# Turning both heads of 72 attention units on VectorE, and reordering the halves' difference, the sums and the statistics, in a fused top-k attention and feed-forward kernel

## The chip, the cores and the metric

The kernel runs on one core of one Trainium2 chip. The metric is the device time of one execution in microseconds, the median of three runs. Names of engines: TensorE (PE in the profile, PEld for its weight loads), VectorE (DVE), ScalarE (ACT), GpSimd (POOL), SyncE (SP, which here issues nearly all transfers).

## What is computed

Top-k attention over 8 batches x 8 heads, 576 positions, 64 columns a head, and on its output a normalised two-layer network without further weights on the residual:

```python
scores = (1/sqrt(64)) * q @ k.T
kth = the 32nd largest score of each row
attn = softmax(where(scores >= kth, scores, -1e9))
x = attn @ v                      # (8, 8, 576, 64) -> (8, 576, 512)
xn = (x - mean(x)) / sqrt(var(x) + 1e-6) * g_ln
out = x + relu(xn @ w_ch1) @ w_ch2   # 512 -> 2048 -> 512
```

All of it is float32.

## The kernel before

**Units and steps.** Work is cut into 160 *units*: 128 queries (or the last 64, a "rest" unit that carries both heads in its 128 partitions) of one pair of heads of one batch. A batch has 20 units. From batch 2 on they come in groups of a pair of heads: units 0, 1 and the rest unit, for each of the four pairs; then units 2 and 3 for each pair. The program is a hand-written order: a loop over steps n, and in each step every engine gets its part of several units at once. In step n TensorE makes the scores of unit n+1, VectorE selects the top 32 of unit n, ScalarE masks unit n-1, and unit n-2 (`ex`) is exponentiated (`weigh`, line 452), turned and put into the group's buffer `pt`. One step after a group's last unit was turned, `values` (lines 563 and 570) multiplies `pt` with V; `place` scales and stores the result as rows of x (line 579), `stats` (lines 629 to 638) centres the rows, and the second network starts on them. Each engine takes its instructions in this written order.

**Selection.** From unit 8 on a unit is *halved*: `halve` (lines 375 to 377) compares the two halves of 288 scores of each row. VectorE writes the larger of each pair to `hi`, GpSimd the smaller to `lo`, by integer arithmetic on the bit patterns: a + b first, then minus `hi`. `lo` has one buffer, `hi` two. `select_halved` then takes the top 8 of `lo` twice (line 390, in part 0), appends them to `hi`, and takes the top 8 of `hi` four times (line 398, `match_replace` in line 385): once in part 1, once in part 2, twice in part 3. In a step the order on VectorE is: part 0 for unit n, part 1, `halve` of unit n+1, part 2, part 3. So part 0 of the next step is what reads `lo`. `sc`, the scores, has four buffers: the buffer that unit n-2 used is filled again with the scores of unit n+2, in step n+1 (line 335).

**Turning.** The product with V needs the weights transposed: keys in the partitions. TensorE does this by `transpose` of four 128 x 128 pieces of a head into PSUM (line 505), and ScalarE copies them to `pt` (line 517 for head 0, line 521 for head 1). The last 64 columns of both heads go the same way (lines 538 and 539). In 72 units (from batch 2 on, every unit that is neither a rest unit nor the last of its group; `moved`) head 1 takes another way: `move` (lines 482 to 489) lets VectorE turn 32 x 32 blocks of `e` into the old score buffer, stores that to HBM with one transfer and loads it back in four, rearranged, so that whole columns lie in the right partitions. The half of `pt` for head 1 is laid out in blocks of 32 queries for this (`ptB`). `move` stands after part 0 of the selection, and so ScalarE exponentiates head 1 first in these steps.

**The second network.** Its matmuls (`hidden`, line 680, and `project`, line 697) are items of a queue `todo`. At fixed places of a step `fill` takes so many from it as the step's `share` allows. Up to step 17 (`CONVERTING`), while the weights are still being converted from 64-bit numbers, the share is worked out from estimated costs (`dve_cost` less `pe_cost`); after that it is what is left to do, spread evenly over the steps up to the next block of rows.

**Small parts.** `prepare` (lines 436 and 437) makes the exponential's bias from the largest and the 32nd score: on VectorE up to unit 16, on GpSimd afterwards. Line 932 turns a group's sums into reciprocals. Line 188 shifts bits of the weights. Line 304 turns q and k. Line 710 on GpSimd adds the residual.

Of the kernel before, what the change touches and what calls it, by code (L numbers as in the profile page):

```python
# [10 lines left out]
ALU = mybir.AluOpType  # L11
FP32 = mybir.dt.float32
U32 = mybir.dt.uint32
I32 = mybir.dt.int32
# [7 lines left out]
J = 4  # L22
# [7 lines left out]
def kernel(  # L30
# [41 lines left out]
    nc = tc.nc  # L72
    P = nc.NUM_PARTITIONS
    B, H, S, D = q.shape
# [3 lines left out]
    JP = J * P  # L78
    R = S - JP
    NHP = H // 2  # L80
    scale = 1.0 / float(D) ** 0.5
# [281 lines left out]
    def halve(u):  # L363

        nt = len(u.tiles)  # L370
        u.lo = lopool.tile([P, 2, HALF], FP32, tag="lo", name="lo")
        u.hi = hipool.tile([P, 2, HALF + TOP_K // 2], FP32, tag="hi", name="hi")
        a, b = u.sc[:, 0:nt, 0:HALF], u.sc[:, 0:nt, HALF:S]
        lo, hi = u.lo[:, 0:nt], u.hi[:, 0:nt, 0:HALF]
        nc.gpsimd.tensor_tensor(lo.bitcast(I32), a.bitcast(I32), b.bitcast(I32), ALU.add)  # L375
        nc.vector.tensor_tensor(hi, a, b, ALU.max)  # L376
        nc.gpsimd.tensor_tensor(  # L377
            lo.bitcast(I32), lo.bitcast(I32), hi.bitcast(I32), ALU.subtract
        )

    def select_halved(u, i):
        nt = range(len(u.tiles))
# [46 lines left out]
    def prepare(u):  # L429

        nt = len(u.tiles)
        u.bias = small.tile([P, 2], FP32, tag="bias", name="bias")
        b = u.bias[:, 0:nt]

        engine = nc.vector if u.i < CONVERTING else nc.gpsimd
        engine.tensor_tensor(b, u.thr[:, 0:nt, 7], u.top[:, 0:nt, 0], ALU.subtract)  # L436
        engine.tensor_scalar(b, b, scale, 0.0, ALU.mult, ALU.add)  # L437

    def mask(u, t):
        if u.e is None:  # L440
# [5 lines left out]
    def weigh(u, t):  # L446
        g = u.group
        if g.den is None:
            g.den = denpool.tile([P, 2 * J + 1], FP32, tag="den", name="den")
        col = 2 * u.qt + t  # L450
        u.weighed += 1
        nc.scalar.activation(  # L452
            u.e[:, t], u.e[:, t], AF.Exp, bias=u.bias[:, t : t + 1], scale=-scale / SLOPE,
            accum_out=g.den[:, col : col + 1],
        )
        if u.rest:
            den = g.den[:, 2 * J : 2 * J + 1]
        elif u.weighed == 2 and u is [x for x in g.units if not x.rest][-1]:
            whole = [qt for qt in g.qts if qt < J]
            den = g.den[:, 2 * whole[0] : 2 * whole[-1] + 2]  # L460
            g.sums = den
        else:
            return
        nc.scalar.activation(den, den, AF.Copy, bias=DEN_EPS)

    def place_of(u):

        g = u.group  # L470
        if g.pt is None:
            g.pt = ptpool.tile([P, 2 * J + 1, GQ], FP32, tag="pt", name="pt")
            g.ptB = g.pt[:, J : 2 * J].rearrange("p c n -> p (c n)").rearrange(
                "p (i c n) -> p i c n", c=J, n=32
            )
        return sum(P for x in g.qts if x < u.qt)

    def move(u):

        i0 = place_of(u) // 32  # L480
        t = u.sc[:, 1, 0:JP]
        nc.vector.transpose(
            t.rearrange("p (j c n) -> p j c n", j=P // 32, c=J),
            u.e[:, 1, R:S].rearrange("p (c j k) -> p j c k", c=J, k=32),
        )
        hbm = hbmpool.tile([P, JP], FP32, tag="turned", name="turned")
        nc.sync.dma_start(hbm[:], t)
        for j in range(P // 32):
            nc.sync.dma_start(
                u.group.ptB[j * 32 : (j + 1) * 32, i0 : i0 + P // 32].rearrange(  # L490
                    "k i c n -> k i (c n)"
                ),
                hbm[:, j * P : (j + 1) * P].rearrange("(i k) x -> k i x", k=32),
            )

    def turn(u):

        g = u.group
        q0 = place_of(u)
        i0 = q0 // 32  # L500

        def part(t):
            ps = turned()
            for c in range(J):
                nc.tensor.transpose(  # L505
                    ps[:, c * P : (c + 1) * P], u.e[:, t, c * P + t * R : (c + 1) * P + t * R],
                    ident[:],
                )
            if u.rest:
                both = ps[:].rearrange("p (c h n) -> p h c n", h=2, n=R)  # L510
                nc.scalar.copy(g.pt[:, 0:J, q0 : q0 + R], both[:, 0])
                nc.scalar.copy(
                    g.ptB[:, i0 : i0 + R // 32],
                    both[:, 1].rearrange("p c (i n) -> p i c n", n=32),
                )
            elif t == 0:
                nc.scalar.copy(  # L517
                    g.pt[:, 0:J, q0 : q0 + P], ps[:].rearrange("p (c n) -> p c n", n=P)
                )
            else:  # L520
                nc.scalar.copy(
                    g.ptB[:, i0 : i0 + P // 32],
                    ps[:].rearrange("p (c i n) -> p i c n", c=J, n=32),
                )

        def last():
            ps = turned()
            if u.rest:
                nc.tensor.transpose(ps[0:R, 0:P], u.e[:, 0, JP:S], ident[:])
                nc.tensor.transpose(ps[:, P : 2 * P], u.e[:, 0, JP - R : S], ident[:])  # L530
                for h in range(2):
                    nc.scalar.copy(
                        g.pt[h * R : (h + 1) * R, 2 * J, q0 : q0 + R],
                        ps[h * R : (h + 1) * R, h * (P + R) : h * (P + R) + R],
                    )
            else:
                ends = u.e[:].rearrange("p t n -> p (t n)")[:, JP : JP + P]
                nc.tensor.transpose(ps[:, 0:P], ends, ident[:])
                nc.scalar.copy(g.pt[:, 2 * J, q0 : q0 + P], ps[:, 0:P])

        heads = [0] if u.moved else range(len(u.tiles))
        return [lambda t=t: part(t) for t in heads] + [last]

    xs, xps, rs, oTr, dr = {}, {}, {}, {}, {}
# [13 lines left out]
    def values(g):  # L558
        vb = g.job.v
        av = brief("av")  # L560
        for c in range(J):
            for h in range(2):
                nc.tensor.matmul(  # L563
                    av[h * D : (h + 1) * D, 0 : g.nq],
                    vb[:, h * J + c, :],
                    g.ptB[:, 0 : g.nq // 32, c, :] if h else g.pt[:, c, 0 : g.nq],
                    start=(c == 0),
                    stop=False,
                )
# [266 lines left out]
    def pe_cost(n):  # L836
        c = 0.0
        if at(n + 1):
            c += 1.25 if at(n + 1).rest else 1.5
        ex, g = after(n)  # L840
        if ex:
            c += 0.67 if ex.rest else 0.55 if ex.moved else 1.0
        if g:
            c += 0.6 + 7.8e-3 * g.nq
        return c
# [54 lines left out]
    for n in range(END):  # L900
# [12 lines left out]
        quick = ex.group if last and ex.group.quick else None  # L913

        moved = ex is not None and ex.moved
        order = (1, 0) if moved else (0, 1)
        sent, stores[:] = stores[:], []

        if ex and not early:
            weigh(ex, order[0])  # L920
# [12 lines left out]
        if n == gives_first:  # L933
            for blk, i in rows_of.pop(n):
                blk.stats(i)
# [7 lines left out]
            weights(n, 0)  # L943
        fill()
        if ex and len(ex.tiles) > 1 and not early:
            weigh(ex, order[1])
        fill()
        if parts and not moved:
            parts[0]()
# [15 lines left out]
        fill()  # L965
        if mk and not early:
            mask(mk, int(mk.moved))
# [6 lines left out]
        if moved:  # L974
            parts[0]()
        elif len(parts) > 2:
# [13 lines left out]
        if parts:  # L990
            parts[-1]()
        if mk and len(mk.tiles) > 1 and not early:
            mask(mk, 1 - int(mk.moved))
# [62 lines left out]
```

## Time and profile before

The median of three runs is 1667.66 us (1666.44 to 1667.72). The profiled execution spans 1666.8 us.

| engine | busy us | share of the span | instructions |
|---|---|---|---|
| TensorE | 1574.1 | 94% | 7113 |
| VectorE | 1464.5 | 88% | 4476 |
| ScalarE | 1077.2 | 65% | 2759 |
| GpSimd | 664.0 | 40% | 879 |

The groups that the change touches (mean of one, count, and what the engine last waited for in front of them):

| line, engine | what | count | mean ns | idle before, us |
|---|---|---|---|---|
| 376, VectorE | maximum of the halves, 128 x 576 | 120 | 1038 | 5.5, for ScalarE's scores |
| 376, VectorE | the same for rest units, 128 x 288 | 32 | 445 | 0.0 |
| 375, GpSimd | a + b, 128 x 576 | 120 | 1436 | 267.0, most of it for scores and a free `lo` |
| 377, GpSimd | minus `hi`, 128 x 576 | 120 | 1425 | 106.6, for the maximum |
| 505, TensorE | transposition, 128 x 128 | 864 | 285 | 38.2, for the exponential |
| 517, ScalarE | head 0 from PSUM to `pt`, 128 x 512 | 128 | 583 | 62.1, for TensorE |

A row's mean is the time of one instruction as the profile shows it. TensorE's instructions overlap, so a mean of 285 ns for a transposition isn't what a further one costs; that is read from the chain of work in order of time. Idle time before a group only matters on the engine that sets the pace. Store and load of the turned weights (lines 487 and 489) take a median of 2.0 us each from issue to landing, 256 KB and four times 64 KB.

### The profile page before, as it was taken

Reading aid. Unit: us, or ns where it says so; the run is one execution under the profiler, and the core shown is the slowest. Engines: PE = TensorE matmul, PEld = TensorE weight load, DVE = VectorE, ACT = ScalarE, POOL = GpSimd, SP = SyncE. Lnnn points to the kernel's source line nnn. Section 1 sums busy time; section 2 is a strip of 40 time slices with the busy share of each in tenths; the row PEclk is TensorE's granted clock in tenths of the full one; section 3 lists DMA queues with packets and bytes.
Section 4 is the critical chain, followed back from the end, with each engine's and each line's share of the span. In section 5 each row is a group of like instructions: output and inputs, shape, how many; then the busy total and the mean of one; then the engine's idle time right before and its main releaser. Section 6 shows DMA issues by size and latency. Waiting matters only on the chain.

```text
span 1666.8 us, 25284 instructions
## 1 busy us (share of the span) xinstructions
PE 1574.1 (94%) x7113; PEld 955.1 (57%) x7113; DVE 1464.5 (88%) x4476; ACT 1077.2 (65%) x2759; POOL 664.0 (40%) x879
## 2 busy tenths in 40 slices
PE   3568989989999999999999999999999999999998
PEld 1346556566555575755547575745547575755564
DVE  5998999999999999999999999899998999998000
ACT  5677967767666776767666675767666676665310
POOL 5567854343433434343343434343243433333010
PEclk9758999999999999999999999999999999999999
DMA  7423333001331133213231233112331132111000
GB/s 176 100 64 108 89 58 59 22 14 27 76 81 51 53 76 81 65 54 69 59 86 51 55 73 83 52 54 70 65 89 44 53 81 74 52 46 47 26 13 13
DMA packets 301203, 104.58 MB, mean 63 GB/s; under 512 B 246276, under 2 KB 283144, under 8 KB 301064
## 3 DMA queue, kind: packets, MB, share of 16 engines
q1 hardware_dynamic: 296328, 102.39, 24.4%
q10 hardware_dynamic: 4736, 0.59, 0.3%
q8 instruction: 57, 0.93, 0.2%
q14 instruction: 82, 0.67, 0.1%
HBM read 74.58 MB, written 28.31 MB: 62 GB/s over the span
## 4 chain that ended last, share of the span: by engine, by line
PE 71%; DVE 21%; issue 4%; ACT 2%; POOL 1%; DMA 1%; ACTq 0%; POOLq 0%; DVEq 0%; SPq 0%
PE hps L680 25%; PE ops L697 24%; PE scps L354 8%; PE av L563 6%; DVE m L398 5%; DVE hi L385 4%; PE tp L505 4%; DVE hi L390 2%; DVE m L416 2%; PE av L570 2%; DVE w L423 2%; DVE lo L385 1%; DVE hi L376 1%; DVE size L188 1%; PE tp L667 1%
## 5 line engine op out<-in xcount | busy, mean ns | idle before, releaser
L680 PE MATMUL hps<-xT,w 128*128 128x256 f32 (+1 forms) x2048 | 550.0, 411 | 2.7 <-ACT xT L672 2.3
L697 PE MATMUL ops<-w,h 128*128 128x512 f32 x1152 | 546.1, 599 | 0.0
L398 DVE MAX8 m<-hi 128x8 f32<-128x304 f32 x1088 | 460.7, 458 | 2.3
L680 PEld LDWEIGHTS hps<-xT,w 128*128 128x128 f32 x2048 | 372.1, 191 | 108.5 <-issue 17.3
L385 DVE MATCH_REPLACE8 hi<-m,hi 128x304 f32<-128x304 f32 x816 | 368.0, 456 | 0.0
L375 POOL TENSOR_TENSOR lo<-sc 128x576 int32<-128x576 int32 (+1 forms) x152 | 197.7, 1301 | 316.3 <-ACT sc L335 156.9
L697 PEld LDWEIGHTS ops<-w,h 128*128 128x128 f32 x1152 | 200.2, 191 | 169.9 <-issue 164.6
L377 POOL TENSOR_TENSOR lo<-lo,hi 128x576 int32<-128x576 int32 (+1 forms) x152 | 196.8, 1295 | 141.9 <-DVE hi L376 139.7
L354 PE MATMUL scps<-kT,qT 64*128 64x288 f32 (+3 forms) x1344 | 217.4, 433 | 32.4 <-DVE qT L304 20.9
L335 ACT COPY sc<-scps 128x288 f32<-128x288 f32 x576 | 199.2, 409 | 62.3 <-PE scps L354 51.0
L442 ACT ACTIVATE e<-sc,m 128x576 f32<-128x576 f32 x288 | 224.3, 779 | 9.7 <-DVE m L398 6.2
L452 ACT ACTIVATE e<-e,bias 128x576 f32<-128x576 f32 x288 | 224.6, 780 | 2.9 <-DVE bias L437 2.5
L390 DVE MAX8 hi<-lo 128x8 f32<-128x288 f32 x544 | 221.8, 443 | 2.6 <-POOL lo L377 1.5
L354 PEld LDWEIGHTS scps<-kT,qT 64*128 64x128 f32 (+1 forms) x1344 | 122.4, 181 | 146.6 <-issue 56.2
L505 PEld LDWEIGHTS tp<-ident,e 128*128 128x128 f32 x864 | 110.9, 147 | 115.9 <-ACT e L452 51.7
L505 PE MATMUL tp<-ident,e 128*128 128x128 f32 x864 | 138.1, 285 | 38.2 <-ACT e L452 37.9
L692 ACT ACTIVATE h<-hps 128x256 f32<-128x256 f32 (+1 forms) x256 | 105.9, 414 | 96.5 <-PE hps L680 93.8
L436 POOL TENSOR_TENSOR bias<-m,m 128x2 f32<-128x2 f32 (+1 forms) x143 | 27.8, 195 | 303.6 <-DVE m L398 303.6
L563 PE MATMUL av<-pt,vb 128*64 128x256 f32 (+2 forms) x1088 | 146.7, 413 | 0.0
L376 DVE TENSOR_TENSOR hi<-sc 128x576 f32<-128x576 f32 (+1 forms) x152 | 138.8, 913 | 5.5 <-ACT sc L335 5.5
L385 DVE MATCH_REPLACE8 lo<-hi,lo 128x288 f32<-128x288 f32 x272 | 118.2, 440 | 0.0
L517 ACT COPY pt<-tp 128x512 f32<-128x512 f32 x128 | 74.6, 583 | 62.1 <-PE tp L505 60.5
(79 smaller groups left out, 1295.0 us busy)
## 6 DMA issues: line engine op xcount, KB each, us to landing
turned<-sc SPq DMA_DIRECT2D x72, 256.0 KB, 2.0
pt<-turned SPq DMA_DIRECT2D x288, 64.0 KB, 2.0
vb<-in_v_dram SPq DMA_DIRECT2D x136, 128.0 KB, 2.5
raw<-in_moe_w_ch_dram SPq DMA_DIRECT2D x32, 512.0 KB, 4.0
kin<-in_k_dram SPq DMA_DIRECT2D x128, 72.0 KB, 2.5
qin<-in_q_dram SPq DMA_DIRECT2D x120, 72.0 KB, 2.5
out_dram<-o SPq DMA_DIRECT2D x32, 256.0 KB, 2.2
ends<-in_v_dram SPq DMA_DIRECT2D x136, 16.0 KB, 2.2
```

The source lines that it names most:

```text
L335: nc.scalar.copy(u.sc[:, t, s * HALF : (s + 1) * HALF], made[s][t][:, 0:HALF])
L354: nc.tensor.matmul(ps[i * R : i * R + ql, o : o + width], qT[r, q0 : q0 + ql], kT[r, k0 : k0 + width], start=True, stop=True,)
L375: nc.gpsimd.tensor_tensor(lo.bitcast(I32), a.bitcast(I32), b.bitcast(I32), ALU.add)
L385: nc.vector.match_replace(x[:, t], m[:, t, :], x[:, t], LOWEST)
L390: nc.vector.max(u.hi[:, t, o : o + 8], u.lo[:, t])
L398: nc.vector.max(m[:, t, :], u.hi[:, t])
L442: nc.scalar.activation(u.e[:, t], u.sc[:, t], AF.Prelu, bias=u.thr[:, t, 7:8], scale=-1.0, alpha=SLOPE)
L452: nc.scalar.activation(u.e[:, t], u.e[:, t], AF.Exp, bias=u.bias[:, t : t + 1], scale=-scale / SLOPE, accum_out=g.den[:, col : col + 1],)
L505: nc.tensor.transpose(ps[:, c * P : (c + 1) * P], u.e[:, t, c * P + t * R : (c + 1) * P + t * R], ident[:],)
L563: nc.tensor.matmul(av[h * D : (h + 1) * D, 0 : g.nq], vb[:, h * J + c, :], g.ptB[:, 0 : g.nq // 32, c, :] if h else g.pt[:, c, 0 : g.nq], ...
L680: nc.tensor.matmul(ps["h"][:, 0:N], w1[:, c, f * P : (f + 1) * P], xT[0][:, c, 0:N], start=(c == 0), stop=(c == NC - 1),)
L697: nc.tensor.matmul(ps[i][:], hT[f][:, i * P : (i + 1) * P], w2[:, f, :], start=(f == 0), stop=(f == NF - 1),)
```

## The change

Four things are changed together.

- `move` turns both heads of the 72 units: two transpositions on VectorE instead of one, one store of 512 KB instead of 256 KB, eight loads instead of four. The four transpositions of head 0 on TensorE and its copy on ScalarE go. `pt` now has the block layout for both heads, so the copies and the product with V use it for head 0 as well. This takes work from TensorE, which has the second network to do.
- `move` stands later in the step: after part 1 and `halve`, between the maximum and part 2. So the exponentials and masks keep their plain order, head 0 first. The reciprocals go to the same place, and the statistics behind part 2.
- GpSimd computes a - `hi` first and then adds b. So neither of its two instructions can start before VectorE's maximum is done; before, a + b could.
- Up to unit 16 `prepare` makes the bias in one VectorE instruction for each head tile, instead of two for both.

The estimate of TensorE's cost for a moved unit becomes 0.15 instead of 0.55; it is used up to step 17 only.

```diff
-        nc.gpsimd.tensor_tensor(lo.bitcast(I32), a.bitcast(I32), b.bitcast(I32), ALU.add)
         nc.vector.tensor_tensor(hi, a, b, ALU.max)
         nc.gpsimd.tensor_tensor(
-            lo.bitcast(I32), lo.bitcast(I32), hi.bitcast(I32), ALU.subtract
+            lo.bitcast(I32), a.bitcast(I32), hi.bitcast(I32), ALU.subtract
         )
+        nc.gpsimd.tensor_tensor(lo.bitcast(I32), lo.bitcast(I32), b.bitcast(I32), ALU.add)
...
-        engine = nc.vector if u.i < CONVERTING else nc.gpsimd
-        engine.tensor_tensor(b, u.thr[:, 0:nt, 7], u.top[:, 0:nt, 0], ALU.subtract)
-        engine.tensor_scalar(b, b, scale, 0.0, ALU.mult, ALU.add)
+        if u.i < CONVERTING:
+            for t in range(nt):
+                nc.vector.tensor_scalar(
+                    b[:, t : t + 1], u.thr[:, t, 7:8], u.top[:, t, 0:1], scale,
+                    ALU.subtract, ALU.mult,
+                )
+            return
...
-        t = u.sc[:, 1, 0:JP]
-        nc.vector.transpose(
-            t.rearrange("p (j c n) -> p j c n", j=P // 32, c=J),
-            u.e[:, 1, R:S].rearrange("p (c j k) -> p j c k", c=J, k=32),
-        )
-        hbm = hbmpool.tile([P, JP], FP32, tag="turned", name="turned")
-        nc.sync.dma_start(hbm[:], t)
+        for t in range(2):
+            nc.vector.transpose(
+                u.sc[:, t, 0:JP].rearrange("p (j c n) -> p j c n", j=ni, c=J),
+                u.e[:, t, t * R : t * R + JP].rearrange("p (c j k) -> p j c k", c=J, k=32),
+            )
+        hbm = hbmpool.tile([P, 2, JP], FP32, tag="turned", name="turned")
+        nc.sync.dma_start(hbm[:], u.sc[:, :, 0:JP])
+        for j in range(ni):
+            for t in range(2):
+                nc.sync.dma_start(
+                    u.group.blocks[j * 32 : (j + 1) * 32, t, i0 : i0 + ni].rearrange(
...
-        heads = [0] if u.moved else range(len(u.tiles))
+        heads = () if u.moved else range(len(u.tiles))
...
-                    g.ptB[:, 0 : g.nq // 32, c, :] if h else g.pt[:, c, 0 : g.nq],
+                    g.blocks[:, h, 0 : g.nq // 32, c, :],
...
         if u:
             select(u, 0)
-        if moved:
-            move(ex)
...
-        for den in recips.pop(n, []):
-            nc.vector.reciprocal(den, den)
...
         if nxt and nxt.halved:
             halve(nxt)
+        for den in recips.pop(n, []):
+            nc.vector.reciprocal(den, den)
+        if moved:
+            move(ex)
...
-        for blk, i in rows_of.pop(n, []):
-            blk.stats(i)
...
         if u:
             select(u, 2)
+        for blk, i in rows_of.pop(n, []):
+            blk.stats(i)
```

More of the change, by code (lines that the diff above doesn't have):

```diff
@@ L433, in prepare @@
         b = u.bias[:, 0:nt]
[L435 to L437 removed]
+        if u.i < CONVERTING:
[5 more added lines that the diff above has]
+            return
+        nc.gpsimd.tensor_tensor(b, u.thr[:, 0:nt, 7], u.top[:, 0:nt, 0], ALU.subtract)
+        nc.gpsimd.tensor_scalar(b, b, scale, 0.0, ALU.mult, ALU.add)
     def mask(u, t):
@@ L472, in place_of @@
             g.pt = ptpool.tile([P, 2 * J + 1, GQ], FP32, tag="pt", name="pt")
-            g.ptB = g.pt[:, J : 2 * J].rearrange("p c n -> p (c n)").rearrange(
-                "p (i c n) -> p i c n", c=J, n=32
+            g.blocks = g.pt[:, 0 : 2 * J].rearrange("p c n -> p (c n)").rearrange(
+                "p (h i c n) -> p h i c n", h=2, c=J, n=32
             )
-        return sum(P for x in g.qts if x < u.qt)
+        return sum(P for x in g.qts if x < u.qt) // 32
     def move(u):
-        i0 = place_of(u) // 32
-        t = u.sc[:, 1, 0:JP]
-        nc.vector.transpose(
-            t.rearrange("p (j c n) -> p j c n", j=P // 32, c=J),
-            u.e[:, 1, R:S].rearrange("p (c j k) -> p j c k", c=J, k=32),
-        )
-        hbm = hbmpool.tile([P, JP], FP32, tag="turned", name="turned")
-        nc.sync.dma_start(hbm[:], t)
[L488 to L493, printed above, removed]
-            )
+        i0 = place_of(u)
+        ni = P // 32
+        for t in range(2):
+            nc.vector.transpose(
+                u.sc[:, t, 0:JP].rearrange("p (j c n) -> p j c n", j=ni, c=J),
+                u.e[:, t, t * R : t * R + JP].rearrange("p (c j k) -> p j c k", c=J, k=32),
+            )
+        hbm = hbmpool.tile([P, 2, JP], FP32, tag="turned", name="turned")
[4 more added lines that the diff above has]
+                    u.group.blocks[j * 32 : (j + 1) * 32, t, i0 : i0 + ni].rearrange(
+                        "k i c n -> k i (c n)"
+                    ),
+                    hbm[:, t, j * P : (j + 1) * P].rearrange("(i k) x -> k i x", k=32),
+                )
     def turn(u):
         g = u.group
-        q0 = place_of(u)
-        i0 = q0 // 32
+        i0 = place_of(u)
+        q0 = i0 * 32
         def part(t):
@@ L510, in part @@
                 both = ps[:].rearrange("p (c h n) -> p h c n", h=2, n=R)
[L511 to L519, printed above, removed]
+                for h in range(2):
+                    nc.scalar.copy(
+                        g.blocks[:, h, i0 : i0 + R // 32],
+                        both[:, h].rearrange("p c (i n) -> p i c n", n=32),
+                    )
             else:
                 nc.scalar.copy(
-                    g.ptB[:, i0 : i0 + P // 32],
+                    g.blocks[:, t, i0 : i0 + P // 32],
                     ps[:].rearrange("p (c i n) -> p i c n", c=J, n=32),
@@ L841, in pe_cost @@
         if ex:
-            c += 0.67 if ex.rest else 0.55 if ex.moved else 1.0
+            c += 0.67 if ex.rest else 0.15 if ex.moved else 1.0
         if g:
@@ L915 @@
         moved = ex is not None and ex.moved
-        order = (1, 0) if moved else (0, 1)
         sent, stores[:] = stores[:], []
         if ex and not early:
-            weigh(ex, order[0])
+            weigh(ex, 0)
         if nxt:
@@ L945 @@
         if ex and len(ex.tiles) > 1 and not early:
-            weigh(ex, order[1])
+            weigh(ex, 1)
         fill()
@@ L966 @@
         if mk and not early:
-            mask(mk, int(mk.moved))
+            mask(mk, 0)
         if g:
@@ L973 @@
         fill()
-        if moved:
-            parts[0]()
-        elif len(parts) > 2:
+        if len(parts) > 2:
             parts[1]()
@@ L992 @@
         if mk and len(mk.tiles) > 1 and not early:
-            mask(mk, 1 - int(mk.moved))
+            mask(mk, 1)
         fill()
```

## The prediction

> **What bounds the kernel now.** I first cut the span into stretches in the view of windows. From 428 us, where the first moved unit is turned, to 1527 us, the columns are stretch, length, then busy time of TensorE, its weight loads, VectorE, ScalarE and GpSimd:
>
> ```profile
> 428.00:700.00 272.00, 269.82 (x1230) 163.07 (x1229) 262.81 (x823) 181.50 (x475) 107.01 (x154) 0.99 0.27 69
> 700.00:1000.00 300.00, 299.23 (x1367) 179.05 (x1366) 287.41 (x897) 203.00 (x525) 111.78 (x157) 1.00 0.25 64
> 1000.00:1300.00 300.00, 298.93 (x1347) 177.17 (x1346) 283.88 (x887) 197.37 (x515) 113.80 (x163) 1.00 0.26 66
> 1300.00:1527.00 227.00, 226.45 (x1037) 138.33 (x1035) 211.03 (x660) 148.91 (x387) 84.80 (x120) 1.00 0.21 56
> ```
>
> TensorE is busy for 1094.4 of these 1099 us, VectorE for 1045.1. Busy TensorE may be a flattering picture, so I looked at the chain of work inside the stretch, in order of time (start, length, what). It runs from one matmul group to the next with no gap:
>
> ```profile
> 602.47 1.49 PE hps L680 x6
> 603.96 0.44 PE tp L505 x4
> 604.40 2.59 PE hps L680 x12
> ```
>
> So TensorE sets the pace, and four transpositions cost it 0.44 us. The waits inside 428 to 1530 (who, for whom, us in total, times, longest) say the same:
>
> ```profile
> DVE sc L482 <- ACT e L452: 46.0, 18, 7.8
> DVE hi L390 <- POOL lo L377: 1.5, 1, 1.5
> ```
>
> VectorE waits only where it has run ahead of ScalarE, which follows TensorE; it has some 5% to spare. After 1527 us VectorE has almost nothing left (17.9 us busy of 140) and TensorE works off the rest of the second network. Before 428 us it is the other way round: VectorE is busy for 185.9 of the 188 us from 240 to 428.
>
> One VectorE cost is not its own. In the timeline (start, length, instruction) the maximum of the two score halves takes 0.74 us alone, and 1.92 us where GpSimd's addition began 0.1 us earlier:
>
> ```profile
> 913.84 0.74 DVE L376 TENSOR_TENSOR hi<-sc 128x576 f32<-128x576 f32 x1
> ...
> 922.37 1.41 POOL L375 TENSOR_TENSOR lo<-sc 128x576 int32<-128x576 int32 x1 [3.18 <-ACT sc L335]
> 922.47 1.92 DVE L376 TENSOR_TENSOR hi<-sc 128x576 f32<-128x576 f32 x1
> ```
>
> **What the Trainium skill says.** "SBUF — State Buffer", Who interferes with whom: VectorE and GpSimd share a pair of ports; a VectorE instruction with two SBUF inputs and a GpSimd instruction that reads SBUF exclude each other, and the later one blocks until the first ends. The trace agrees (0.74 against 1.92 us above). The same section lets an instruction with one SBUF input outside the two-port modes run undisturbed: line 482's transpositions took 0.680 to 0.712 us throughout. "Perfetto Trace Analysis", Identifying the Most-Contended Engine, warns that matmul busy time misjudges TensorE, hence the look at the chain. "DMA: Bandwidth & Descriptors", Anatomy of one DMA, prices a transfer at about 2 us plus bytes over 436 GB/s; the 256 KB store of line 487 landed in 2.0 us here.
>
> **The change, part by part.**
>
> *Head 0 of the 72 units leaves TensorE.* Each loses four transpositions, 0.44 us, and a ScalarE copy of 0.58 us (line 517), which lay beside other work. 70 of the 72 units are turned inside the stretch: 70 x 0.44 = 30.8 us off TensorE. The amount of filling work per step doesn't change, since after step 17 the share comes from what is left to do and not from the cost that the diff lowers.
>
> *VectorE turns it instead.* The groups by form give the price of one, and that of the small bias instructions:
>
> ```profile
> L482 DVE STREAM_TRANSPOSE sc<-e 128x512 f32<-128x512 f32 x72 | 50.3, 698 | 59.7 <-ACT e L452 59.4
> L436 DVE TENSOR_TENSOR bias<-m,m 128x2 f32<-128x2 f32 x16 | 10.7, 670 | 0.6
> ```
>
> 70 x 0.694 = 48.6 us more on VectorE.
>
> *GpSimd starts after the maximum.* Then its two instructions of the same unit can't hold the maximum up. Line 376 took 109.6 us in the stretch (93 whole units, 23 half ones); undisturbed it would be 93 x 0.745 + 23 x 0.445 = 79.5 us, so 30 us were blocking. GpSimd has other two-input work (line 710); I leave 3 us for meetings with it and take 27 off. The price is a later `lo`: 0.14 + 1.41 + 0.08 + 1.41 = 3.04 us after the maximum instead of some 1.55. After a whole unit's maximum VectorE has 3.97 us of selection before it reads `lo`; in the step of a short unit 2.47 us, but there both transpositions (1.39 us) now come between, which makes 3.86. Only in four steps of batch 1 (halves at 330, 355, 380 and 405 us), where nothing is moved, does VectorE wait, 0.57 us each: 2.3 us.
>
> *Sum of the stretch.* VectorE: 1045.1 + 48.6 - 27 = 1067 us. TensorE: 1099 - 30.8 = 1068 us. The statistics now come after one more part of the selection, 1.65 us later; at the row tiles that are turned at once (TensorE's line 667 at 1127.38 us, GpSimd done at 1126.50) the slack of 0.9 us is used up, so I add 3 us: 1071. The two engines become equal. They are coupled through ScalarE both ways, and equal engines stall each other a little; before, with 5% between them, TensorE lost 4.6 us. I add 6 us, an estimate: 1077 us, 22 less than now.
>
> *The new waits.* The turning moves from about 2.3 us into a step to about 5.3 us, behind the second exponential; it was behind the first. ScalarE ended a second exponential at 914.4 us in a step where VectorE would reach its second transposition at 915.4, so VectorE may lead by 1 us there, and behind it are the next two parts of the selection. On the other side, the scores of two steps on are copied into the buffer that the store reads. Take the step of 836 us: maximum at 839.7, transpositions done at 841.9, store of 512 KB landed at 844.6 by the skill's price (844.0 if it took 2.1 us as half the size did, 846.1 if twice that); ScalarE copies scores at 846.02. There is 1.4 us to spare, between 2.0 and -0.1. What queues behind that copy are the exponentials and the evacuations that TensorE's banks wait for. The eight transfers into `pt` (8 x 0.44 us of issue, 2.0 us to land) end at 850.1; the product with V reads it at 854.5. I cost both at nothing beyond the 6 us.
>
> *Before 428 us*, where VectorE sets the pace: the two bias instructions on VectorE (11.8 + 3.1 us for lines 436 and 437) become 33 of about 0.17 us, 5.6 us. Of the 9.3 us saved I count 6: the savings after 147 us, the last point where VectorE waited there for TensorE's first block (4.45 us). Blocking of line 376 is 4.9 us, of which 4.4 go. Against it stand the 2.3 us above and about 1.7 us at 341 us, where TensorE already waits 4.8 us for the statistics. Net 6 us. The reciprocals only change place (0.13 us each); the end after 1527 us is TensorE's and loses 2 x 0.44 us, which the later statistics may take back: nothing.
>
> 1667.7 - 22 - 6 = 1639.7 us, say 1640.
>
> **The rivals.** *TensorE's saving shows in full*: no stalls between equal engines, 1667.7 - 30.8 - 6 = 1631. For it: TensorE lost only 0.4% before. Against it: VectorE's spare 5% is gone.
>
> *VectorE becomes the bound*: GpSimd's other work keeps half of the blocking alive, so VectorE needs 1045.1 + 48.6 - 15 = 1079 us, and its waits for the second exponential keep some 10 of the present 46 us: 1089, a gain of 10; with 4 before 428 us the time is 1654. For it: the work moves to an engine that is already at 95%.
>
> *Slower*: the store, twice as large and 3 us later, comes behind the score copies. If it holds up ScalarE and then TensorE by 0.7 us in each of the 70 steps, that is +49: 1667.7 - 6 - 30.8 + 3 + 49 = 1683. Shorter TensorE steps and longer VectorE steps eat the margin above by 1.1 us a step until something gives, which speaks for it; that ScalarE is idle for a third of the stretch and that three banks of the second network lie between it and TensorE's stall speaks against.
>
> **How the numbers follow.** The forecast gets 0.47, full saving 0.15, VectorE as the bound 0.22, slower 0.16. The forecast is the likeliest case, 1640. The range goes from 1629, just below the full saving, to 1669, which takes in the third case and the unchanged time; out of it are most of the slower case and a little at the bottom, together under 0.2. Faster: the first three without their edges, 0.82; within 0.2%: 0.04; slower: 0.14.
>
> **What would show it.** Line 376 at a mean near 0.75 us for 128x576 instead of 1.04. Line 505 with 576 matmuls instead of 864. VectorE's and TensorE's busy time within 1% of each other from 428 us on, VectorE's waits for ScalarE's `e` below 46 us, and the stretch near 1077 us. VectorE waiting for GpSimd's `lo` only in batch 1. I am wrong if score copies wait for the `turned` transfer, if TensorE has new gaps before line 505 or 354, or if line 376 stays long.

## The result and the profile after

The changed kernel takes 1691.05 us (median of four runs, 1690.19 to 1694.62). The kernel before takes 1667.05 us beside it (four runs, 1666.01 to 1667.72). The ratio is 1.0149, with a 95% interval of 1.0131 to 1.0166: the change makes the kernel 24 us slower, where 27 us faster was forecast. The measured time lies above the range as well. The profiled execution spans 1688.4 us.

First, the same stretches in the view of windows, now of the kernel after (stretch, length, then busy time of TensorE, its weight loads, VectorE, ScalarE and GpSimd, the granted clock, the share of the transfer engines, GB/s):

```profile
428.00:700.00 272.00, 251.15 (x1063) 146.06 (x1062) 250.43 (x783) 159.80 (x425) 96.71 (x140) 0.97 0.36 98
700.00:1000.00 300.00, 291.08 (x1268) 170.41 (x1267) 286.51 (x905) 188.95 (x496) 112.18 (x157) 0.99 0.33 93
1000.00:1300.00 300.00, 289.88 (x1250) 169.35 (x1249) 281.90 (x877) 184.86 (x488) 110.90 (x160) 1.00 0.37 99
1300.00:1527.00 227.00, 224.15 (x1020) 137.33 (x1018) 220.90 (x701) 144.94 (x386) 85.94 (x123) 1.00 0.33 92
```

VectorE is not the bound: it is idle for 21.6 of the first 272 us. TensorE's idle time, at most 2.2 us in any of these stretches before, is now 20.9, 8.9, 10.1 and 2.9 us (length less busy time). Both engines wait, so something else holds them, and the view of waits names it (who, for whom, us in total, times, longest; from 413 to 1550 us, the five longest of TensorE):

```profile
PE av L567 <- DMA vb<-in_v_dram: 13.5, 8, 3.9
PE av L567 <- issue: 7.2, 7, 2.5
PE av L567 <- DMA ends<-in_v_dram: 5.6, 9, 1.7
PE tp L671 <- POOL r L642: 5.0, 3, 1.8
PE av L567 <- DMA qin<-in_q_dram: 5.0, 1, 5.0
```

Line 567 is the product with V (line 563 before). Before the change it waited for nothing in this part of the kernel. Now it waits for `vb` and `ends`, which are V itself: transfers that the diff doesn't touch. The rows with "issue" (no releaser that the profile shows) and with `qin` are waits of the same product; together the four rows of line 567 make 31.3 us, and all four are gone once V's loads are moved (first experiment). The chain of work in order of time, which ran from matmul to matmul without a gap before, now goes through them (start, length, what):

```profile
670.87 0.04 issue
670.92 0.50 SPq L278
...
672.00 0.50 SPq L278
672.49 0.04 issue
672.54 2.82 DMA vb<-in_v_dram
675.36 0.35 issue
675.71 5.06 PE av L567 x16
```

The chain comes from SyncE's queue: SyncE issues the loads of q (line 278), then V, then V takes 2.8 us to land, and only then does TensorE start. It had ended its scores at about 672.0.

Next, SyncE's own timeline around such a place (start, length, instruction), before:

```profile
838.20 0.34 SPq L487 DMA_DIRECT2D turned<-sc  x1
840.28 1.73 SPq L489 DMA_DIRECT2D pt<-turned  x4
842.10 0.38 SPq L712 DMA_DIRECT2D out_dram<-o  x1
842.58 2.07 SPq L278 DMA_DIRECT2D kin<-in_k_dram  x4
844.75 2.29 SPq L278 DMA_DIRECT2D qin<-in_q_dram  x4
847.09 0.50 SPq L290 DMA_DIRECT2D vb<-in_v_dram  x1
...
848.82 0.52 SPq L294 DMA_DIRECT2D ends<-in_v_dram  x1
```

and after:

```profile
661.22 0.57 SPq L494 DMA_DIRECT2D turned<-sc  x1
664.61 3.63 SPq L497 DMA_DIRECT2D pt<-turned  x8
668.34 2.00 SPq L278 DMA_DIRECT2D kin<-in_k_dram  x4
670.43 2.06 SPq L278 DMA_DIRECT2D qin<-in_q_dram  x4
672.54 0.50 SPq L290 DMA_DIRECT2D vb<-in_v_dram  x1
...
674.29 0.52 SPq L294 DMA_DIRECT2D ends<-in_v_dram  x1
```

SyncE issues strictly in the written order. The loads into `pt` wait until the store has landed, and everything behind them waits too: eight loads of k and q, then the four of V, written at the end of the step. Before, the last of V was issued at 849.34 and TensorE's product started at 854.43: 5.1 us in hand, where V's loads need a median of 2.1 to 2.5 us to land (the last of them, `ends` of head 1, is read only by the matmuls of line 574, behind the 16 of line 567). After, the queue is later in two ways. `move` stands some 2.4 us later in the step (the first transposition starts 2.3 us after the beginning of part 0 of the selection before, 4.7 us after the change; medians), and the store has to wait for one more transposition, 0.7 us. And from the store's issue to the end of the loads into `pt` it takes 7.0 us instead of 3.8, because the store of 512 KB lands in 3.1 us (2.0 for 256 KB) and eight loads take 3.63 us to issue where four took 1.73. In the place shown the last of V is issued at 674.8, 0.9 us before the product starts, and the product has already waited 3.7 us.

The changed pieces themselves do what was forecast (groups of the kernel after: line, engine, operation, count, busy us, mean ns, idle before):

```profile
L375 DVE TENSOR_TENSOR hi<-sc 128x576 f32<-128x576 f32 x120 | 92.9, 774 | 19.5 <-ACT sc L335 19.0
L489 DVE STREAM_TRANSPOSE sc<-e 128x512 f32<-128x512 f32 x144 | 95.9, 688 | 60.8 <-ACT e L458 60.7
L437 DVE TENSOR_SCALAR bias<-m,m 128x1 f32<-128x1 f32 x33 | 5.5, 202 | 0.0
```

The maximum takes 774 ns instead of 1038, a transposition 688 ns, a bias instruction 202 ns; TensorE's transpositions went from 864 to 576.

For what follows I cut the profile at the same two groups of scores (line 354) in each kernel. In this section, which takes in nearly all moved units, the times are 1103.9 us before (422.26 to 1526.19) and 1133.4 us after (415.34 to 1548.70). So after is 6.9 us ahead when the section starts and loses 29.5 us in it; the rest, about 140 us, is the same within 1 us.

### The profile page after: what moved, and what is told of

Its sections match the earlier page's. It is cut to its first block, busy times and chain, and to the rows that moved or that the text cites. A ratio compares the mean times of both kernels' runs of the same rounds, so it can differ in the third digit from the quotient of the medians.

```text
span 1688.4 us, 24932 instructions
## 1 busy us (share of the span) xinstructions
PE 1562.0 (93%) x6825; PEld 934.4 (55%) x6825; DVE 1473.3 (87%) x4547; ACT 1037.4 (61%) x2687; POOL 663.3 (39%) x879
## 4 chain that ended last, share of the span: by engine, by line
PE 43%; DVE 39%; issue 5%; DMA 4%; ACT 3%; SPq 3%; POOL 2%; DVEq 0%; ACTq 0%; POOLq 0%
PE hps L684 17%; DVE m L398 11%; PE ops L701 11%; DVE hi L385 10%; PE av L567 6%; DVE hi L390 6%; PE scps L354 4%; DVE lo L385 3%; DVE hi L375 3%; DVE sc L489 2%; PE av L574 2%; SPq L278 1%; DMA ends<-in_v_dram 1%; PE tp L513 1%; DVE m L416 1%
## 5 line engine op out<-in xcount | busy, mean ns | idle before, releaser
L684 PE MATMUL hps<-xT,w 128*128 128x256 f32 (+1 forms) x2048 | 543.6, 410 | 2.4 <-ACT xT L676 2.0
L701 PE MATMUL ops<-w,h 128*128 128x512 f32 x1152 | 540.6, 599 | 0.0
L376 POOL TENSOR_TENSOR lo<-sc,hi 128x576 int32<-128x576 int32 (+1 forms) x152 | 196.9, 1295 | 509.6 <-DVE hi L375 230.9
L354 PE MATMUL scps<-kT,qT 64*128 64x288 f32 (+3 forms) x1344 | 218.3, 432 | 29.5 <-DVE qT L304 21.4
L379 POOL TENSOR_TENSOR lo<-lo,sc 128x576 int32<-128x576 int32 (+1 forms) x152 | 194.9, 1282 | 11.9
L567 PE MATMUL av<-pt,vb 128*64 128x256 f32 (+2 forms) x1088 | 165.3, 424 | 35.6 <-DMA vb<-in_v_dram 13.5
L489 DVE STREAM_TRANSPOSE sc<-e 128x512 f32<-128x512 f32 x144 | 95.9, 688 | 60.8 <-ACT e L458 60.7
L567 PEld LDWEIGHTS av<-pt,vb 128*64 128x64 f32 x1088 | 83.9, 145 | 110.9 <-issue 55.6
L579 ACT COPY oT<-av 128x256 f32<-128x256 f32 (+2 forms) x68 | 26.3, 386 | 175.2 <-PE av L574 175.2
L513 PE MATMUL tp<-ident,e 128*128 128x128 f32 x576 | 94.5, 290 | 35.5 <-ACT e L458 35.4
L375 DVE TENSOR_TENSOR hi<-sc 128x576 f32<-128x576 f32 (+1 forms) x152 | 108.2, 712 | 19.5 <-ACT sc L335 19.0
```

The source lines that it names most:

```text
L354: nc.tensor.matmul(ps[i * R : i * R + ql, o : o + width], qT[r, q0 : q0 + ql], kT[r, k0 : k0 + width], start=True, stop=True,)
L376: nc.gpsimd.tensor_tensor(lo.bitcast(I32), a.bitcast(I32), hi.bitcast(I32), ALU.subtract)
L379: nc.gpsimd.tensor_tensor(lo.bitcast(I32), lo.bitcast(I32), b.bitcast(I32), ALU.add)
L567: nc.tensor.matmul(av[h * D : (h + 1) * D, 0 : g.nq], vb[:, h * J + c, :], g.blocks[:, h, 0 : g.nq // 32, c, :], start=(c == 0), stop=False,)
L684: nc.tensor.matmul(ps["h"][:, 0:N], w1[:, c, f * P : (f + 1) * P], xT[0][:, c, 0:N], start=(c == 0), stop=(c == NC - 1),)
L701: nc.tensor.matmul(ps[i][:], hT[f][:, i * P : (i + 1) * P], w2[:, f, :], start=(f == 0), stop=(f == NF - 1),)
```

## The experiments

**Theory 1**: V's loads, last in SyncE's queue, come too late for the product with V, and the turning itself is worth what I forecast. **Theory 2**: the two engines, now equally full, stall each other through ScalarE, and V's wait is only where that shows. All times are medians. The kernel before took 1666.3 to 1667.1 us beside them.

| kernel | us | ratio to before (95%) |
|---|---|---|
| after | 1691.05 | 1.0149 (1.0131 to 1.0166) |
| V's loads first | 1642.24 | 0.9854 (0.9838 to 0.9870) |
| V's loads between `pt` and k, q | 1644.98 | 0.9869 (0.9855 to 0.9884) |
| V's loads on ScalarE's queue | 1652.43 | 0.9912 (0.9897 to 0.9927) |
| one head turned, in the late place | 1665.10 | 0.9989 (0.9983 to 0.9996) |
| before, with the order on GpSimd and the bias | 1658.87 | 0.9952 (0.9937 to 0.9967) |
| before, with the bias alone | 1662.39 | 0.9973 (0.9963 to 0.9984) |
| after, with GpSimd's old order | 1707.09 | 1.0237 (1.0215 to 1.0260) |
| V's loads first, with GpSimd's old order | 1658.75 | 0.9957 (0.9943 to 0.9971) |
| V's loads first, statistics earlier | 1642.68 | 0.9855 (0.9840 to 0.9869) |

### V's loads ahead of the turning

```diff
             nc.vector.reciprocal(den, den)
+        if n > EARLY and mk and mk is units[mk.job.last]:
+            load_values(mk.job)
         if moved:
             move(ex)
...
-        for x in (u if n < EARLY else None, mk if n > EARLY else None):
-            if x and x is units[x.job.last]:
-                load_values(x.job)
+        if n < EARLY and u and u is units[u.job.last]:
+            load_values(u.job)
```

> The changed kernel with one thing moved: the loads of V for a group (lines 290 and 294) are issued ahead of the step's turning, instead of at the end of the step. Theory 1, SyncE's queue: the V loads stood behind the store of the turned weights, its landing (3.1 us) and eight loads (3.7 us), and TensorE waited for them at line 567; from 428 us on the steps with a product with V lost some 60 us. Then these waits go and the time falls from 1691 to 1635 to 1650, where VectorE and TensorE are equal. Theory 2, VectorE is the bound (twice the turning, and the wait for the second exponential): the time stays above 1680. Theory 3, the store of the turned weights holds up the copies of the scores: also above 1680.

It took 1642.24 us: 49 us less than after, 25 us less than before. Theory 1 holds. The third theory of the expectation doesn't: ScalarE's score copies wait for the store of the turned weights even longer here (12.8 us in ten places, 420 to 1510 us) than in after (5.0 us in four, 413 to 1550 us), and the time falls all the same. SyncE's timeline of this kernel shows V issued ahead of the store of its step:

```profile
669.50 0.43 SPq L290 DMA_DIRECT2D vb<-in_v_dram  x1
...
671.16 0.52 SPq L294 DMA_DIRECT2D ends<-in_v_dram  x1
671.77 0.58 SPq L494 DMA_DIRECT2D turned<-sc  x1
674.89 3.67 SPq L497 DMA_DIRECT2D pt<-turned  x8
```

The product of that group starts at 681.49, 9.8 us after V's last issue ended. TensorE's waits for V are gone; what is left in the view of waits (420 to 1510 us) is small:

```profile
PE tp L671 <- POOL r L642: 7.3, 4, 2.5
PE tp L671 <- POOL x L642: 1.8, 2, 1.6
PE av L567 <- ACT sc L335: 1.8, 1, 1.8
PE av L567 <- DMA pt<-turned: 1.7, 3, 1.3
```

Of the 49 us, 46.5 lie in the section (1133.4 against 1086.9 us). TensorE's idle time in it goes from 44.5 to 15.7 us, which is 28.8. The other 17.7 are longer matmuls, as the view of windows has them: 1088.9 us busy against 1071.2 with one matmul between them. The product with V carries most. The groups of 320 columns, from 413 to 1549 us, after and then with V first:

```profile
L567 PE MATMUL av<-pt,vb 128*64 128x320 f32 x400 | 71.9, 471 | 24.5 <-DMA vb<-in_v_dram 6.3 <-issue 5.2 <-DMA qin<-in_q_dram 5.0
```

```profile
L567 PE MATMUL av<-pt,vb 128*64 128x320 f32 x400 | 60.8, 438 | 4.3 <-ACT sc L335 1.8 <-DMA pt<-turned 1.7 <-ACT e L448 0.8
```

After a long wait these 16 matmuls take 5.06 us (above, at 675.71) or 5.30 (at 447.12), and 2.37 us undisturbed. In the same places the granted clock falls (windows of 10 us of after; the clock is the third number from the end):

```profile
590.00:600.00 10.00, 5.92 (x28) 3.40 (x25) 8.69 (x30) 1.63 (x6) 4.49 (x6) 0.83 0.50 95
...
670.00:680.00 10.00, 6.31 (x27) 3.21 (x27) 8.58 (x28) 3.12 (x9) 5.02 (x7) 0.71 0.53 109
```

Over the product at 675.71 alone it is half:

```profile
675.71:680.77 5.06, 5.06 (x17) 2.16 (x17) 2.90 (x8) 0.00 (x0) 2.58 (x2) 0.50 0.19 59
```

The Trainium skill, "TensorE: Matmul & The Clock Gate", What's actually happening, says that the clock is gated down after an idle window of about 3.4 us. The trace agrees in part: three of the four dips in this section follow waits of 5.0, 3.9 and 3.7 us, but the fourth follows one of 2.3 us, while one of 2.5 us has none. So the length of a single wait doesn't decide it alone. Summed over windows of 10 us, one minus the clock makes 10.2 us in after's section and 1.7 us with V first. So a wait for V costs its own length and, if it is long, up to about 3 us of slow matmuls behind it. The remaining 9 us of longer busy time lie in the products with V too: in all, line 567 is busy for 120.3 us in after's section and for 101.7 us with V first. In 17 products of after the clock stays at 1.00, and still 16 matmuls take 2.6 to 3.5 us instead of 1.95 (256 columns) or 2.37 (320). In one of them TensorE starts the two matmuls of head 0 that come first in the program, and then waits again before those of head 1, whose V is loaded last (the profile names `ends`, which is loaded between the two heads' `vb`). The timeline of after, and the same group with V first:

```profile
615.75 0.62 PE L567 MATMUL av<-pt,vb 128*64 128x256 f32 x2
616.73 1.91 PE L567 MATMUL av<-pt,vb 128*64 128x256 f32 x14 [0.36 <-DMA ends<-in_v_dram]
```

```profile
599.89 1.95 PE L567 MATMUL av<-pt,vb 128*64 128x256 f32 x16
```

How much of this is waiting that the modelled ends of matmuls show as work, I can't say.

### One head, in the late place

```diff
-        for t in range(2):
+        for t in (1,):
...
-        heads = () if u.moved else range(len(u.tiles))
+        heads = (0,) if u.moved else range(len(u.tiles))
...
```

The store is 256 KB and there are four loads again; TensorE turns head 0, at the place in the step where it did before.

> The changed kernel, but only head 1 is turned by VectorE as in the kernel before (one store of 256 KB, four loads), head 0 on TensorE again; the turning stays in its new place in the middle of the step, and all other parts stay. It tells the later place from the doubling. Theory 1: the place alone makes the V loads about 3 us later, the doubling about 3 us more (1 us of landing, 1.8 us of issue); so part of the waits at line 567 stays, and TensorE has its 31 us back: 1665 to 1685. Theory 2: the doubling is what costs, so the time is about that of before less the 6 us at the start: 1658 to 1663.

It took 1665.10 us, just inside the range of theory 1, but not for its reason: the waits for V are absent, and TensorE's longest wait in the section is 2.1 us, once. Still, the margin has shrunk. In 22 groups of the section loads of k and q stand ahead of V. There V's last issue ends 5.1 us ahead of the product in the kernel before (median; 1.3 to 6.9), 2.7 us in this one (0.8 to 4.1), and 0.6 us in after, where the product has already waited. So the later place uses up about half of the margin, and only with the second head's store and loads does V come too late. GpSimd's order and the bias, worth 8 us on the kernel before (next experiment), are in this kernel too, and it gains only 2: so the place, with the later reciprocals and statistics, seems to cost some 6 us without any wait for V. I haven't separated these.

### GpSimd's order and the bias on the kernel before; the bias alone

```diff
-        nc.gpsimd.tensor_tensor(lo.bitcast(I32), a.bitcast(I32), b.bitcast(I32), ALU.add)
         nc.vector.tensor_tensor(hi, a, b, ALU.max)
         nc.gpsimd.tensor_tensor(
-            lo.bitcast(I32), lo.bitcast(I32), hi.bitcast(I32), ALU.subtract
+            lo.bitcast(I32), a.bitcast(I32), hi.bitcast(I32), ALU.subtract
         )
+        nc.gpsimd.tensor_tensor(lo.bitcast(I32), lo.bitcast(I32), b.bitcast(I32), ALU.add)
...
+        if u.i < CONVERTING:
+            for t in range(nt):
+                nc.vector.tensor_scalar(...)
+            return
...
```

The kernel with the bias alone has the second of these edits only.

> The kernel before with only two parts of the change: GpSimd takes the difference to the larger scores first, and the bias up to unit 16 is made in one VectorE instruction for each head tile. The place of the turning, head 0, sums and statistics stay as before. Line 376's maximum (before: 1.04 us on average) should take 0.75 us. All theories: TensorE sets the pace from 428 us on, so the 27 us that VectorE saves there show as longer waits, and only the 6 to 9 us of the first 428 us count: 1658 to 1662. If it gains over 15 us, VectorE was more of a bound than I read.

> The kernel before with one part of the change only: the bias up to unit 16 in one VectorE instruction for each head tile. With the order of the difference as well it took 1658.9 us, 8.1 less than before. My working for the first 428 us gave 6 us to the bias and 4.4 - 2.3 us to the order, so about 1661 here. If the order carries most of it (the waits before line 375 fall away also after 428 us), this stays above 1664.

Both together take 8.1 us off (1658.87 against 1666.97); the bias alone takes 3.9 off (1662.39 against 1666.30). So the order is worth about 4 us there. The maximum got 258 ns shorter, 120 times, which is 31 us of VectorE, and most of it turned into waiting (view of waits of the kernel with both, 420 to 1540 us):

```profile
DVE sc L488 <- ACT e L458: 58.1, 23, 9.1
DVE hi L390 <- POOL lo L379: 12.0, 24, 1.5
```

VectorE wasn't the bound, so it just waited longer: 58.1 us for the exponential where it had been 46.0, and 12.0 for `lo` where it had been 1.5.

### The old order on the kernel after

```diff
+        nc.gpsimd.tensor_tensor(lo.bitcast(I32), a.bitcast(I32), b.bitcast(I32), ALU.add)
         nc.vector.tensor_tensor(hi, a, b, ALU.max)
         nc.gpsimd.tensor_tensor(
-            lo.bitcast(I32), a.bitcast(I32), hi.bitcast(I32), ALU.subtract
+            lo.bitcast(I32), lo.bitcast(I32), hi.bitcast(I32), ALU.subtract
         )
-        nc.gpsimd.tensor_tensor(lo.bitcast(I32), lo.bitcast(I32), b.bitcast(I32), ALU.add)
```

> The changed kernel with GpSimd's order of before (a + b first, then minus the larger). Theory 1: while TensorE waits for V, VectorE has time to spare; the blocking comes back (27 us on VectorE) and shows only in part: 1690 to 1705. Theory 2, VectorE is the bound: all of it shows, 1715 or more.

It took 1707.09 us, 16 us more than after; the four runs spread from 1701.45 to 1710.15. That lies between the two theories and decides nothing by itself. Longer waits for V don't explain it: in the profiled run, the fastest of the four and 11 us longer than after's, the four rows of waits at line 567 that made 31.3 us in after make 31.6 us (413 to 1565 us). One minus the clock, summed over windows of 10 us, comes to some 15 us in the section, 5 more than in after. The rest stays open.

### The old order with V first

```diff
+        if n > EARLY and mk and mk is units[mk.job.last]:
+            load_values(mk.job)
         if moved:
             move(ex)
```

as with V first, and in `halve` the edit just shown.

> The kernel with V first (1642 us) and GpSimd's order of before (a + b first). It prices the blocking of the maximum in a kernel in which VectorE has no time to spare (busy 293 to 296 of 300 us). My working: VectorE gets 20 to 27 us more from 428 us on and sets the pace, 4 us more before that, less 2 us of waits in batch 1: 1660 to 1672. Rival: as in the kernel before, VectorE's blocking is hidden: 1645.

It took 1658.75 us, 16.5 more than with V first alone, a little less than expected. With the old order the maximum takes 941 ns, with the new one 775 (groups of these two kernels, the old order first):

```profile
L376 DVE TENSOR_TENSOR hi<-sc 128x576 f32<-128x576 f32 x120 | 112.9, 941 | 16.7 <-ACT sc L335 16.5
```

```profile
L375 DVE TENSOR_TENSOR hi<-sc 128x576 f32<-128x576 f32 x120 | 93.0, 775 | 15.4 <-ACT sc L335 15.4
```

120 times 166 ns are 19.9 us, against 16.5 us of time. The same edit was worth about 4 us on the kernel before, where TensorE set the pace. "SBUF — State Buffer", Who interferes with whom, has the mechanism (a VectorE instruction with two SBUF inputs, such as this maximum, and a GpSimd instruction that reads SBUF exclude each other), and the trace agrees: 941 against 775 ns. What the shorter maximum is worth differs between the two kernels; that this is because VectorE has no time to spare with V first is my reading.

### V's loads in the same place, on another queue

```diff
-            nc.sync.dma_start(
+            nc.scalar.dma_start(
                 vb[:, hh * J : (hh + 1) * J, :],
...
-            nc.sync.dma_start(
+            nc.scalar.dma_start(
                 job.ends[hh * R : (hh + 1) * R, hh * D : (hh + 1) * D],
```

> The changed kernel with the loads of V (lines 290 and 294) at the same place of the program, but issued by ScalarE instead of SyncE. Nothing else moves. It tells SyncE's order from the place in the step. Theory 1, SyncE's queue: V no longer stands behind the turned weights and the loads of k and q, the waits at line 567 go, and the time is near that of the kernel with V first (1642 us), with some us for four issues on ScalarE for each group: 1640 to 1655. Rival: what helped was issuing V half a step earlier, whatever the queue; or the transfers themselves are slow because more bytes move: then above 1675.

It took 1652.43 us, 38.6 less than after. Place in the step, number and bytes of all transfers are those of after; only who issues four of them differs. So it is the order in SyncE's queue, not the load on the transfer engines. "DMA: Bandwidth & Descriptors", Issuing engines are not separate DMA queues, calls the time that an issue takes on its engine "usually small relative to the DMA itself". Taken one by one that fits, 0.45 us against 2.0 us to land; but issues on one queue add up, and eight of them took 3.63 us. The 10 us that are missing to V first are most likely lost on ScalarE, whose exponentials now queue behind those issues and their waits:

```profile
L458 ACT ACTIVATE e<-e,bias 128x576 f32<-128x576 f32 x288 | 224.4, 779 | 95.5 <-DMA ends<-in_v_dram 31.7 <-issue 23.4 <-DMA turned<-sc 12.5
```

Its idle time in front of the exponential is 95.5 us; in after it was 0.6.

### V between the turned weights and k, q

```diff
         if moved:
             move(ex)
+        if n > EARLY and mk and mk is units[mk.job.last]:
+            load_values(mk.job)
```

and the loads at the end of the step go, as with V first.

> The changed kernel with the loads of V on SyncE behind the turned weights as before, but ahead of the eight loads of k and q (line 278, some 4.1 us of issue) that follow them in a third of the steps. The lost time lies in the groups of units 0, 1 and rest, where these loads are. Theory 1: V is issued 4 us earlier there, against lost 2 to 6 us a group: most of it comes back, 1642 to 1660. Rival: the turned weights alone (store, landing, eight loads) make V late: 1670 or more.

It took 1644.98 us, within 3 us of V first. So the enlarged transfers alone don't ruin V; together with the 4.1 us of issues for k and q between them they do. The view of waits names V once for TensorE, 0.8 us.

### V first, statistics earlier

```diff
             halve(nxt)
+        for blk, i in rows_of.pop(n, []):
+            blk.stats(i)
...
             select(u, 2)
-        for blk, i in rows_of.pop(n, []):
-            blk.stats(i)
```

> The kernel with V first (1642 us) and the statistics back ahead of part 2 of the selection, right behind the maximum, before reciprocals and turning. There TensorE waited 9.1 us in all for the centred rows at line 671, against none in that stretch before the change. If the later statistics cost what that wait shows: 1632 to 1640. If the waits only move on, because VectorE and TensorE are level: 1641 to 1645.

It took 1642.68 us, no difference to V first. TensorE's waits for GpSimd's rows (line 671) fall from 9.1 to 1.1 us (420 to 1510 us), but its waits for ScalarE rise from 4.8 to 10.6, among them these:

```profile
PE hps L684 <- ACT xT L676: 2.5, 2, 1.7
PE av L567 <- ACT sc L335: 2.0, 2, 1.1
PE scps L354 <- ACT xT L676: 1.8, 1, 1.8
...
PE tp L671 <- POOL r L642: 1.1, 3, 0.6
```

TensorE waits nearly as long as before, for another engine: it has run ahead and meets the next thing that isn't ready. The later statistics cost nothing in this kernel.

## Why the prediction was wrong

- **The failed step** is in "The new waits": "The eight transfers into `pt` (8 x 0.44 us of issue, 2.0 us to land) end at 850.1; the product with V reads it at 854.5. I cost both at nothing beyond the 6 us." The number of 0.44 us was about right (3.63 us for eight), and `pt` was in time (1.7 us of waits for it with V first). The step asked only whether the enlarged transfer arrives itself, and not what is queued behind it on SyncE. Behind it stand k, q and V, and V had 5.1 us in hand, 2.1 to 2.5 of them needed. The later place and the larger transfers took these. Its own step would have shown it: there V's last issue ended 7.3 us behind the last issue into `pt` (842.01 and 849.34 in the timeline of before). Behind loads whose issue ends at 848.1 (850.1 less 2.0) that puts it at about 855.4, an estimate from these lines, and the product starts at 854.5. What was put at nothing costs 49 us (after against V first).
- **The rival "slower"** named 1683 us, nearer than the forecast, but its cause, scores that wait for the store, is not what happened: ScalarE's score copies waited for `turned` 5.0 us in all, in four places. Such waits were also named as a sign of being wrong; they came, but with V first they are longer (12.8 us) in a kernel that is 49 us faster. That its figure is the nearer one is luck. Its chance was too low, since I weighed the store and the loads by their own readers only.
- **The rest of the sum holds** once V is out of the way: V first takes 1642.24 us, where 1640 was forecast. That these are so close is in part luck: the section gains 17.0 us of the forecast 22, and the time before it 8.4 instead of 6. In the section VectorE is busy for 1065.8 us (forecast 1067, for the slightly shorter stretch). TensorE's busy time falls by 28.1 us (1099.4 to 1071.2) instead of 30.8, and its idle time rises by 11.1 (4.6 to 15.7) where 6 for equal engines and 3 for the statistics were allowed.
- **TensorE's 0.44 us a unit**: yes. From one group of scores to the next, the commonest length of a moved step is 10.55 us with V first, and was 10.99 before.
- **Blocking**: the maximum came to 774 ns, near the 0.75 us expected. Put at 27 us of VectorE inside the stretch, it is worth 16.5 us of time with V first.
- **Before the stretch**: 6 us forecast; after is 6.9 us ahead at its start, V first 8.4.
- **VectorE as the bound** didn't come about. In after VectorE waits 45.2 us for the exponential from 428 to 1550 us, with V first 7.8 us (420 to 1510 us); below 46 was the sign I named for my own case, and after meets it barely for another reason.
- **The wait for `lo`**: 2.5 us in the stretch, where none was expected there, and 1.6 us in four places before it, where 2.3 was. The store of 512 KB, put at 2.7 us after the transpositions (841.9 to 844.6), takes 3.1.

Shown by experiment are the order in SyncE's queue as the cause (V first, V on another queue, V ahead of k and q) and that the place alone doesn't suffice (one head). The slow clock behind long waits is read from the trace and not isolated. Open are what costs the one-head kernel its 6 us, why the old order costs 16 us on the kernel after, and how much of the 9 us in the products with V is waiting.

## What to carry to other kernels

When a transfer is enlarged or moved, list what is issued behind it on the same queue up to the next wait, and compare for each the end of its issue with the time its reader needs it; a load that the change doesn't touch can be the first to fail. Put loads that depend on nothing ahead of transfers that wait for data of the same step. What an edit that relieves an engine is worth depends on the kernel around it: the same reorder on GpSimd was worth 4 us in one kernel and 16.5 in the other.

## What the runs showed of the hardware

- In the steps shown the issue of a load took 0.43 to 0.59 us of SyncE, whether it was of 16, 64, 72 or 128 KB. The twenty issues of the step shown, from the first load into `pt` to the last of V, hold SyncE for 10.2 us; each transfer lands a median of 2.0 to 2.4 us after its issue.
- The store of 512 KB takes a median of 3.1 us from issue to landing, the one of 256 KB 2.0 us.
- Waits of TensorE of 3.7 and 5.0 us were followed by products with V of 5.1 and 5.3 us instead of 2.37, at a granted clock of 0.50. A wait of 2.3 us had a dip of the clock behind it too, one of 2.5 us had none.
- With V's loads issued by ScalarE, it was idle for 95.5 us in front of its exponentials instead of 0.6, and the kernel took 10 us more than with V first.
